# Two transformer layers on one core: a new order of the dense matmuls, zero matmuls in idle TensorE time, and smaller first loads

## The chip, the cores and the metric

The kernel runs on one core of a Trainium2 chip. The metric is the device time of one execution in microseconds (us), the median of several runs. A profile of one execution shows what each engine did: TensorE (PE: matmuls; PEld: its weight loads), VectorE (DVE), ScalarE (ACT), GpSimd (POOL) and SyncE (SP, which issues the DMA transfers). In lines of the profile, L672 means line 672 of that kernel's file.

## The reference

Four blocks follow one another on a stream x of 2048 tokens by 512 features: attention, token-mixing MLP, attention, MLP, that is two layers with the same weights.

```python
def _A_ref(x, wqkv, wo):                 # attention: 32 heads of 16, window of 256 tokens
    qkv = (x @ wqkv) ...                 # split in q, k, v per head
    scores = einsum("bhqd,bhkd->bhqk", q, k) * 16 ** -0.5
    mask = (i - j >= 0) & (i - j < 256)
    p = softmax(where(mask, scores, -1e9))
    return (p @ v) ... @ wo
def _B_ref(x, w1, b1, w2, b2):           # MLP over the token axis
    h = layernorm(x)
    u = gelu(einsum("bsd,sf->bdf", h, w1) + b1)      # 2048 tokens -> 1792
    y = einsum("bdf,fs->bds", u, w2) + b2            # 1792 -> 2048 tokens
    return y transposed
x = x + A(layernorm(x));  x = x + B(layernorm(x))
x = x + A(layernorm(x));  x = x + B(layernorm(x))
```

## The kernel before

The kernel is written as a graph of operations. Python code, before anything is compiled, gives each operation an estimated cost, plays the graph through on a simple model of the engines, and so fixes the order of instructions on each engine. The chip then runs those orders, with semaphores for the dependencies. An order is never changed while the kernel runs.

The tokens are worked in four chunks of 512. The steps of a layer are p (normalise, project q, k, v), a (attention), w (output projection), u (part of the first MLP matmul), U (the last part, with GELU):

```python
STEPS = ("p0 p1 a0 p2 w0 u0 a1 p3 w1 u1 a2 w2 u2 a3 w3 U3",
         "p0 p1 a0 p2 w0 a1 p3 w1 u01 a2 w2 u2 a3 w3 U3")
```

The second MLP matmul (y) of layer 0 is part of layer 1's p steps. TensorE takes scores first, then probabilities x V (PV), then dense matmuls by priority, which is their place in the program:

```python
        if e == "tensor":
            for kind in (SCORE, PV):
                c = [(o.prio, t, o) for t, o in est if o.kind == kind and t <= m + self.WINDOW[kind]]
                if c:
                    c.sort(key=lambda x: x[0])
                    return c[0][1], c[0][2]
...
    HOLD = 0.0
    WINDOW = {0: 100.0, 1: 150.0}
    SLACK = {"scalar": 60.0}
...
        STEP = 2                       # dense matmuls of a group that are issued as one operation
        def fprio():
            return 1e6 + len(g.ops)
```

Attention, for each of 4 groups of heads in a chunk, goes through 4 or 5 pieces. A piece is a set of score matmuls into four PSUM banks, two exponentials on ScalarE from PSUM to `pt`, and masks on VectorE. Score banks are limited to 6 of 8, so one and a half pieces fit:

```python
        psum = Pool("psum", 8, {"sc": 6, "small": 3, "big": 6})
...
                    prev_sc[0] = op("tensor", f_sc, reads=[tq] + kk, writes=[sa, sb_], ... kind=SCORE, mode="row", tag="sc")   # L672
                    for u, ts in ((0, sa), (1, sb_)):
                            return e.activation(pt[:, tp.slot, 2 * u:2 * u + 2, 0:n], PS[:, b0:b0 + 2, 0:n],               # L684
                                                ACTF.Exp, scale=SMSCALE)
                        ...                                                                                                 # masks: L697, L700
                op("tensor", f_pv, ... kind=PV, mode="pv", ...)                                                             # L717
```

The last group of heads of the last chunk uses another form of PV (L730). The results go through a normalisation by way of DRAM (cs, scr, rr, rscr, md), which ends in a product on GpSimd (L781).

The projections: K is copied from PSUM to `stg` by VectorE or ScalarE, and GpSimd spreads it to `kbd` in two operations (L604), the form the scores read:

```python
                op(*evac(lambda: stg[:, ts.slot, :], lambda: PS[:, ft.slot, :]), reads=[ft], writes=[ts], prio=-1e4)
                for h in range(2):
                    op("gpsimd", lambda e, h=h: e.tensor_scalar(
                        kbd[:, tk[o].slot, :, h, :], stg[:, ts.slot, :].rearrange("p (s n) -> p s n", n=64),
                        par[:, h:h + 1], 0.0, op0=ALU.mult, op1=ALU.add), ...)
```

Normalisation (`ln_block`): statistics of x (L530, L532) on VectorE, reciprocal root on GpSimd (L535, L537), and `xh_sb` on VectorE (L541). In the last chunk it is done for two tiles of 128 tokens at a time, and the first MLP matmul (L830) and the transposes (L579) wait for it:

```python
            ln_block([4 * m, 4 * m + 1], True)
            ln_block([4 * m + 2, 4 * m + 3], True)
```

The first loads:

```python
        load_x(0, 2)
        load_x(2, 4)
        load_w(1)
        load_w(0)
        load_x(4, 8)
        load_w(2)
        load_x(8, 12)
        load_x(12, 16)
```

Of the kernel before, what the change touches and what calls it, by code (L numbers as in the profile page):

```python
# [7 lines left out]
dt = mybir.dt  # L8
ALU = mybir.AluOpType
# [4 lines left out]
SWITCH = 95.0  # L14
SCORE, PV, DENSE = 0, 1, 2
STEPS = ("p0 p1 a0 p2 w0 u0 a1 p3 w1 u1 a2 w2 u2 a3 w3 U3",
# [24 lines left out]
class Op:  # L41
    __slots__ = ("idx", "eng", "engs", "fn", "cost", "lat", "prio", "deps", "users", "ndeps", "tiles", "start", "end",
                 "done", "seq", "dma", "extra", "kind", "mode", "tag")


class Graph:
# [15 lines left out]
    def op(self, eng, fn, reads=(), writes=(), cost=100.0, lat=None, prio=None, dma=False, after=(), holds=(),  # L62
           kind=DENSE, mode="full", tag=""):
# [6 lines left out]
        o.prio, o.kind, o.mode = prio, kind, mode  # L70
# [88 lines left out]
    def _pick(self, e, cand, ready, free, mode):  # L159
# [8 lines left out]
        for o in cand:  # L168
# [3 lines left out]
            t = max(ready[o.idx], t)  # L172
            if any(tl.slots is None for tl in o.tiles):
# [11 lines left out]
        if e == "tensor":  # L185
            for kind in (SCORE, PV):
                c = [(o.prio, t, o) for t, o in est if o.kind == kind and t <= m + self.WINDOW[kind]]
                if c:
                    c.sort(key=lambda x: x[0])
                    return c[0][1], c[0][2]  # L190
# [8 lines left out]
    HOLD = 0.0  # L199
    WINDOW = {0: 100.0, 1: 150.0}  # L200
    SLACK = {"scalar": 60.0}

    HAM = 3413.3

# [18 lines left out]
    def schedule(self):  # L223
        self.busy, self.rates = {}, [0.5]
# [12 lines left out]
        while left:  # L237
# [8 lines left out]
            m, e, o = best  # L246
            for x in o.engs:
                cand[x].remove(o)
            o.eng = e
            o.fn, o.cost = o.engs[e]  # L250
            self._alloc(o)
# [6 lines left out]
            else:  # L258
                if e == "tensor":
                    o.cost = self._clocked(m, o.cost)  # L260
                o.end = free[e] = m + o.cost
                o.done = o.end + (o.lat if o.lat is not None else self.LAT[e])
# [14 lines left out]
    def emit(self, block):  # L277
# [22 lines left out]
        pending = len(self.ops)  # L300
# [83 lines left out]
def bass_interleave_layers__sliding_block__mixer_token_mlp__prompt_kernel(  # L384
# [18 lines left out]
    NACT = 2  # L403
# [3 lines left out]
    with es:  # L407
# [21 lines left out]
        ident = sb("ident", [P, P])  # L429
        ldm = sb("ldm", [P, 2, 64])  # L430
# [30 lines left out]
        op("gpsimd", lambda e: e.memset(mhalf[:], -0.5), writes=["mhalf"])  # L461

# [7 lines left out]
        def load_x(t0, t1):  # L470
            op("sync", lambda e: e.dma_start(x_sb[:, t0:t1, :], x_src[:, t0:t1, :]),
               writes=[f"x{t}" for t in range(t0, t1)], dma=True, cost=(t1 - t0) * 600, prio=-1e6)

        def load_w(i):
            op("sync", lambda e: e.dma_start(wqkv[:, :, i * 512:(i + 1) * 512], w_src[:, :, i * 512:(i + 1) * 512]),
               writes=[f"w{i}"], dma=True, cost=2600, prio=-1e6)
        load_x(0, 2)
        load_x(2, 4)
        load_w(1)
        load_w(0)  # L480
        load_x(4, 8)
        load_w(2)
# [445 lines left out]
```

The softmax here doesn't subtract the row's maximum and nothing guards it: scores larger than these inputs give would overflow.

## Time and profile before

| | us |
|---|---|
| time, median of 3 runs | 501.48 (497.84 to 502.52) |
| span of the profiled execution | 499.8 |
| TensorE busy | 430.5 |
| VectorE busy | 377.1 |
| ScalarE busy | 321.9 |
| GpSimd busy | 137.0 |
| mean granted TensorE clock | 0.973 |

A busy share is an average over stages that differ. So the page has the span in 40 slices of 12.5 us, with a digit for the busy tenths of each engine in each. Idle times are listed with what ended them: "A <- B: total, times, longest" says how long A stood still until B was done. "issue" means that the profile shows nothing that the engine waited for.

### The profile page before, as it was taken

To read this page: it belongs to the slowest core of one execution; us is meant where nothing else is said; L and a number is where in the kernel's file an instruction comes from. 1 tells how busy PE (TensorE), PEld (TensorE's weight loads), DVE (VectorE), ACT (ScalarE), POOL (GpSimd) and SP (SyncE) were. 2 spreads that over 40 slices of the span, in tenths; PEclk is the share of its full clock that TensorE was granted. 3 is DMA by queue.
4 is the path that set the end of the run, shared out by engine and by line. 5 is a ranking of instruction groups with operands and counts; after the bars stand their busy time and mean duration, and the time that the engine had idled before them with its cause. 6 is when DMAs were issued, how large, how long until landed. Compare 5 with 4: busy or idle time off the path is not lost.

```text
span 499.8 us, 15471 instructions
## 1 busy us (share of the span) xinstructions
PE 430.5 (86%) x6746; PEld 209.0 (42%) x6816; DVE 377.1 (75%) x745; ACT 321.9 (64%) x365; POOL 137.0 (27%) x205
## 2 busy tenths in 40 slices
PE   2998758798859859699999899898889998999997
PEld 1554423344423334244544444345444344444443
DVE  6799957888888867766888878998897678872222
ACT  1788987898789961080598998697988872070000
POOL 3472333315431131102321621561481212100000
PEclk9999988899979979899999999999999999999999
DMA  8944243264326534154037355344534672524663
GB/s 266 216 98 146 100 148 110 95 199 134 104 102 202 176 101 119 39 147 125 24 117 226 113 163 164 111 142 126 162 96 153 200 220 75 147 64 118 197 193 103
DMA packets 91435, 69.23 MB, mean 139 GB/s; under 512 B 16232, under 2 KB 79848, under 8 KB 91368
## 3 DMA queue, kind: packets, MB, share of 16 engines
q1 hardware_dynamic: 91368, 68.25, 45.7%
q8 instruction: 53, 0.87, 0.8%
q14 instruction: 14, 0.11, 0.1%
HBM read 49.42 MB, written 18.32 MB: 136 GB/s over the span
## 4 chain that ended last, share of the span: by engine, by line
PE 50%; DVE 27%; ACT 9%; DMA 7%; POOL 2%; issue 2%; SPq 1%; POOLq 0%
PE PS L830 16%; PE PS L853 15%; ACT pt L684 9%; PE PS L717 5%; PE PS L595 5%; DVE stats L530 4%; PE PS L672 4%; DVE pt L700 3%; DVE xh_sb L541 3%; DVE pt L697 3%; DMA rr<-cs 3%; DVE cs L759 3%; PE PS L791 2%; DMA rscr<-rr 2%; DVE vt L567 2%
## 5 line engine op out<-in xcount | busy, mean ns | idle before, releaser
L684 ACT ACTIVATE pt<-PS 128x1024 bf16<-128x1024 f32 (+1 forms) x304 | 282.9, 1033 | 47.3 <-PE PS L672 43.0
L830 PE MATMUL PS<-xh_sb,w1b 128*128 128x512 bf16 x423 | 103.8, 387 | 17.2 <-DVE xh_sb L541 7.7
L853 PE MATMUL PS<-ub,w2b 128*128 128x512 bf16 x427 | 100.6, 380 | 2.7 <-issue 2.1
L781 POOL TENSOR_TENSOR oT<-md 128x512 bf16<-128x512 f32 x30 | 39.3, 1309 | 154.9 <-DMA md<-rscr 154.8
L672 PE MATMUL PS<-qT,kbd 32*128 32x64 bf16 (+4 forms) x1632 | 61.3, 246 | 19.6 <-ACT pt L684 9.1
L700 DVE TENSOR_TENSOR pt<-pt,ldm 128x1024 bf16<-128x1024 bf16 (+1 forms) x80 | 58.0, 726 | 16.2 <-ACT pt L684 16.1
L830 PEld LDWEIGHTS PS<-xh_sb,w1b 128*128 128x128 bf16 x448 | 40.4, 99 | 68.0 <-DVE xh_sb L541 13.4
L595 PE MATMUL PS<-xhT,wqkv 128*128 128x512 bf16 x239 | 62.5, 393 | 5.4 <-issue 2.8
L853 PEld LDWEIGHTS PS<-ub,w2b 128*128 128x128 bf16 x448 | 41.0, 98 | 50.6 <-issue 4.8
L604 POOL TENSOR_SCALAR kbd<-stg,par 128x512 bf16<-128x512 bf16 x64 | 50.0, 792 | 36.8 <-DVE stg L567 30.5
L672 PEld LDWEIGHTS PS<-qT,kbd 32*128 32x128 bf16 x1632 | 23.5, 93 | 77.8 <-ACT pt L684 52.5
L842 DVE TENSOR_TENSOR ub<-PS,ub 128x512 f32<-128x512 f32 x70 | 47.3, 688 | 10.5 <-PE PS L830 10.1
L858 DVE SCALAR_TENSOR_TENSOR x_sb<-PS,b2col,x_sb 128x512 bf16<-128x512 f32 x32 | 23.9, 748 | 40.1 <-PE PS L853 40.1
L697 DVE TENSOR_TENSOR pt<-pt,ldm 128x512 bf16<-128x512 bf16 (+1 forms) x104 | 43.6, 427 | 9.8 <-ACT pt L684 9.1
L845 ACT ACTIVATE ub<-ub,b1col 128x512 bf16<-128x512 f32 x28 | 19.6, 719 | 45.3 <-DVE ub L842 42.8
L717 PE MATMUL PS<-pt,vt 64*18 64x64 bf16 (+4 forms) x3040 | 42.1, 257 | 7.0 <-ACT pt L684 2.5
L530 DVE BATCH_NORM_STATS2 stats<-x_sb 128x6 f32<-128x512 bf16 x64 | 42.7, 681 | 2.9 <-DMA x_sb<-in_A_x_dram 2.5
L759 DVE COPY cs<-PS 128x512 f32<-128x512 f32 x60 | 38.5, 682 | 6.4 <-PE PS L717 6.2
L717 PEld LDWEIGHTS PS<-pt,vt 64*18 64x18 bf16 x3040 | 32.6, 89 | 19.5 <-ACT pt L684 10.7
L595 PEld LDWEIGHTS PS<-xhT,wqkv 128*128 128x128 bf16 x256 | 22.0, 100 | 32.7 <-issue 7.9
L541 DVE TENSOR_SCALAR xh_sb<-x_sb,agg,rstd 128x512 bf16<-128x512 bf16 x64 | 28.5, 476 | 8.8 <-POOL rstd L537 8.5
L791 PE MATMUL PS<-wo_sb,oT 128*128 128x512 bf16 x121 | 30.9, 381 | 3.7 <-DVE oT L748 1.3
(49 smaller groups left out, 297.4 us busy)
## 6 DMA issues: line engine op xcount, KB each, us to landing
scr<-cs SPq DMA_DIRECT2D x30, 512.0 KB, 3.2
w1b<-in_B_w_dram SPq DMA_DIRECT2D x56, 256.0 KB, 3.2
w2b<-in_B_w_dram SPq DMA_DIRECT2D x16, 896.0 KB, 6.3
md<-scr SPq DMA_DIRECT2D x60, 128.0 KB, 2.8
md<-rscr SPq DMA_DIRECT2D x60, 128.0 KB, 2.8
out_dram<-x_sb SPq DMA_DIRECT2D x16, 128.0 KB, 2.8
wqkv<-in_A_wqkv_dram SPq DMA_DIRECT2D x3, 512.0 KB, 7.7
x_sb<-in_A_x_dram SPq DMA_DIRECT2D x3, 512.0 KB, 9.5
```

The lines of the kernel that those rows point to most:

```text
L530: op("vector", lambda e, t=t: e.bn_stats(stats[:, t, :], x_sb[:, t, :]), reads=[f"x{t}"], writes=[f"st{t}"], cost=dve_cost(512))
L595: mm_group(ft, 4, lambda e, c: e.matmul(PS[:, ft.slot, :], lhsT=wqkv[:, c, which * 512 + o * P:which * 512 + (o + 1) * P], rhs=xhT[:, tx.s ...
L604: op("gpsimd", lambda e, h=h: e.tensor_scalar(kbd[:, tk[o].slot, :, h, :], stg[:, ts.slot, :].rearrange("p (s n) -> p s n", n=64), par[:, ...
L672: last = e.matmul(PS[:, bank(r), c0 * 64:(c0 + nb) * 64], lhsT=kbd[32 * r:32 * r + 32, tkk.slot, jj, :, :].rearrange("p h n -> p (h n)"), ...
L684: return e.activation(pt[:, tp.slot, 2 * u:2 * u + 2, 0:n], PS[:, b0:b0 + 2, 0:n], ACTF.Exp, scale=SMSCALE)
L697: return e.tensor_tensor(v, v, msk.unsqueeze(1).to_broadcast([P, 4, w]), op=ALU.mult)
L700: return e.tensor_tensor(v, v, msk.unsqueeze(1).unsqueeze(1).to_broadcast([P, 4, k, w]), op=ALU.mult)
L717: last = e.matmul(PS[32 * r:32 * r + 18, tO[h].slot, q0 * 64:(q0 + nb) * 64], lhsT=vt[64 * h:64 * h + 64, tvv.slot, jj, 4 * o + r, :], rhs ...
L759: op("vector", lambda e, tO=tO[h], tc=tc, h=h: e.tensor_copy(cs[:, tc.slot, h], PS[:, tO.slot, :]), reads=[tO[h]], writes=[(tc, h)], cost= ...
L830: out_ = e.matmul(PS[:, tu.slot, :], lhsT=w1b[:, tw.slot, s, tt * P:(tt + 1) * P], rhs=xh_sb[:, 4 * m + s, :], start=(n == 0 and s == 0), ...
L842: op("vector", lambda e, tu=tu, ft=ft: e.tensor_tensor(uacc(ft), PS[:, tu.slot, :], uacc(ft), op=ALU.add), reads=[tu] + uk(ft), writes=uk( ...
L853: mm_group(ft, NFT, lambda e, fc: e.matmul(PS[:, ft.slot, :], lhsT=w2b[:, tw.slot, fc, k * P:(k + 1) * P], rhs=uT(fc), start=(fc == 0), st ...
```

## The change

It does the following.

- The dense matmul groups get offsets to their priority from a table (`RANK`), which a search found on the model. The model itself is changed: [...]its windows and slacks are other ones. Dense matmuls are issued in fours instead of twos (singly in the last MLP part).
- 13 zero matmuls run ahead of the first real ones, and more are put where the model sees TensorE idle for long, to keep its clock up. In the order that results there are four of these, all in layer 0.
- x is first loaded in tiles of 128 KB, and the first weights in pieces of 128 KB, so that the first work can start sooner.
- K of chunk 0 in layer 0 goes from PSUM to `kbd` by ScalarE directly (`KACT`).
- The last chunk is normalised one tile at a time.
- Some set-up operations get other priorities and costs.

`EVACT` says the same as `NACT` did. With the values given here `XHP` (normalise on GpSimd), `NTR` and `DTR` (transposes by DMA) and `PVSPLIT` (PV in two parts) leave the kernel as it was.

```diff
-SWITCH = 95.0
+SWITCH = 100.0
+NWARM = 13
+NTR, DTR = 4, 1200
+EVACT = {(0, 0), (0, 1), (1, 0), (1, 1)}
+XHP = set()
+RANK = (
+    0, 0, 453, -32, -93, 0, -132, -49, 69, 0, 0, 0, 0, 0, 0, 0, -49, 7, 0, 52, -55, 0, -56, 46, 35, -50, -11, -39,
 ...  (322 numbers in all)
+KACT = {(0, 0, o) for o in range(4)}
+PVSPLIT = {True: ((0, 4),), False: ((0, 5),)}
 ...
+            if e == "vector" and o.port:
+                t = max(t, self.ported[1])
+            elif e == "gpsimd":
+                t = max(t, self.ported[0])
 ...
-            for kind in (SCORE, PV):
-                c = [(o.prio, t, o) for t, o in est if o.kind == kind and t <= m + self.WINDOW[kind]]
 ...
+            sc = [(o.prio, t, o) for t, o in est if o.kind == SCORE]
+            if sc:
+                _, t, o = min(sc, key=lambda x: x[0])
+                if t <= m + self.WINDOW[o.layer][0]:
+                    return t, o
+            pv = [(o.prio, t, o) for t, o in est if o.kind == PV and t <= m + self.WINDOW[o.layer][1]]
 ...
-    HOLD = 0.0
-    WINDOW = {0: 100.0, 1: 150.0}
-    SLACK = {"scalar": 60.0}
+    HOLD = 300.0
+    WINDOW = ({0: 100.0, 1: 300.0, 2: 50.0}, {0: 50.0, 1: 300.0, 2: 50.0})
+    SLACK = {"scalar": 60.0, "tensor": 300.0}
 ...
+            t = free["tensor"] + (SWITCH if mode != "full" else 0.0)
+            if e == "tensor" and self.warm and t + self.WARM[0] + (SWITCH if o.mode != "full" else 0.0) < m:
 ...  (puts a zero matmul there)
+        zset = op("vector", lambda e: e.memset(zero[:], 0.0), writes=["zero"], cost=120)
+        f_warm = lambda e, t: e.matmul(PS[:, t.slot, :], lhsT=zero[:], rhs=zero[:].unsqueeze(1).to_broadcast([P, 4, P]),
+                                       start=True, stop=True)
+        g.warm = (psum, f_warm, [zset])
+        for i in range(NWARM):
+            tw = Tile(psum, 1, "big")
+            op("tensor", lambda e, tw=tw: f_warm(e, tw), reads=["zero"], writes=[tw], cost=216, prio=-1e6)
 ...
-        load_x(0, 2)
-        load_x(2, 4)
-        load_w(1)
-        load_w(0)
+        load_x(0, 1)
+        load_x(1, 2)
+        load_w(4, 5)
+        load_x(2, 3)
+        load_x(3, 4)
+        load_w(0, 1)
+        load_w(8, 12)
+        load_w(5, 8)
+        load_w(1, 4)
         load_x(4, 8)
-        load_w(2)
         load_x(8, 12)
         load_x(12, 16)
 ...
-        STEP = 2
+        STEP = 4
+
+        groups = [0]
 
         def fprio():
-            return 1e6 + len(g.ops)
+
+            k = groups[0]
+            groups[0] += 1
+            return 1e6 + len(g.ops) + (RANK[k] if k < len(RANK) else 0) + 1e-4 * k
 ...
+                if kact:
+                    for h in range(2):
+                        op("scalar", lambda e, h=h: e.activation(
+                            kbd[:, tk[o].slot, :, h, :], PS[:, ft.slot, :].rearrange("p (s n) -> p s n", n=64), ACTF.Copy,
+                            scale=par[:, h:h + 1]), reads=[ft, ("par", h)], writes=[(tk[o], h)], cost=act_cost(512, 1),
+                           prio=-1e4)
+                    return
 ...
-            ln_block([4 * m, 4 * m + 1], True)
-            ln_block([4 * m + 2, 4 * m + 3], True)
+            for ts in ([[4 * m + i] for i in range(4)] if m == NC - 1 else [[4 * m, 4 * m + 1], [4 * m + 2, 4 * m + 3]]):
+                ln_block(ts, True)
 ...
-            cls = "big" if last else "small"
+            cls, st = ("big", 1) if last else ("small", STEP)
```

## The prediction

> **What bounds the kernel now.** I read the page from the top: the busy shares, then the slices, then the idle times of ScalarE and TensorE by what ended them, and last the stretches where those idle times sit.
>
> Busy shares and slices on the page:
>
> ```profile
> PE 430.5 (86%) x6746; PEld 209.0 (42%) x6816; DVE 377.1 (75%) x745; ACT 321.9 (64%) x365; POOL 137.0 (27%) x205
> ...
> PE   2998758798859859699999899898889998999997
> ...
> ACT  1788987898789961080598998697988872070000
> ...
> PEclk9999988899979979899999999999999999999999
> ```
>
> TensorE (PE) is busy 86% of 499.8 us, so 69 us are idle, and PEclk shows slices in which its clock was lowered. ScalarE (ACT) is dense only in two blocks, slices 1 to 14 and 20 to 32: the exponentials of layer 0 and of layer 1. What ScalarE waited for, over the whole run (total, times, longest):
>
> ```profile
> ACT pt L684 <- PE PS L672: 43.0, 44, 4.1
> ACT ub L845 <- DVE ub L842: 42.8, 3, 21.9
> ACT xhT L569 <- PE PS L579: 19.2, 4, 9.6
> ```
>
> The first line is the one that counts inside attention: the exponential (L684) lacks scores (L672). By stretch it is 10.7 us up to 100 us, 7.9 us from 100 to 184, 10.9 from 246 to 330 and 9.1 from 330 to 415. The other two fall outside attention.
>
> Busy time by stretch (columns: length, PE, weight loads, DVE, ACT, POOL with their counts, PE clock, DMA share, GB/s):
>
> ```profile
> 62.50:75.00 12.50, 7.04 (x186) 3.57 (x180) 6.40 (x12) 11.09 (x14) 4.45 (x6) 0.86 0.46 149
> 137.50:150.00 12.50, 7.05 (x185) 3.29 (x188) 10.17 (x22) 10.69 (x13) 3.92 (x6) 0.73 0.30 104
> 200.00:212.50 12.50, 7.63 (x30) 2.94 (x29) 9.04 (x21) 1.18 (x2) 1.89 (x4) 0.86 0.14 39
> 300.00:312.50 12.50, 11.79 (x243) 6.17 (x247) 10.83 (x21) 11.02 (x13) 1.83 (x3) 1.00 0.56 163
> 462.50:475.00 12.50, 12.39 (x58) 5.65 (x58) 3.00 (x4) 0.00 (x0) 0.00 (x0) 1.00 0.70 199
> ```
>
> So there are three regimes. In layer 0's attention (16.8 to 182 us) ScalarE leads: TensorE is short of filler and now and then half clocked. In layer 1's (242 to 411) PE and ACT are both near full. From 412 to 497 TensorE alone works, warm, and nothing but less work shortens it.
>
> Two more looks, from the timeline of all engines (start, length, what, idle before it and its releaser):
>
> ```profile
> 11.11 5.26 PE L595 MATMUL PS<-xhT,wqkv 128*128 128x512 bf16 x12 [0.52 <-DVE xhT L567]
> 16.76 1.94 ACT L684 ACTIVATE pt<-PS 128x1024 bf16<-128x1024 f32 x2 [1.43 <-PE PS L672]
> ```
>
> ```profile
> 179.41 1.26 POOL L781 TENSOR_TENSOR oT<-md 128x512 bf16<-128x512 f32 x1 [2.15 <-DMA md<-rscr]
> 179.54 1.68 DVE L700 TENSOR_TENSOR pt<-pt,ldm 128x1024 bf16<-128x1024 bf16 x1
> 183.33 0.63 PE L830 MATMUL PS<-xh_sb,w1b 128*128 128x512 bf16 x1 [3.99 <-DVE pt L697]
> 208.06 13.58 PE L830 MATMUL PS<-xh_sb,w1b 128*128 128x512 bf16 x55 [4.87 <-DVE xh_sb L541]
> 221.47 12.25 PE L853 MATMUL PS<-ub,w2b 128*128 128x512 bf16 x55
> ```
>
> The first projections take 438 ns each (5.26 / 12), later ones of the same size 223 ns at most (12.25 / 55; a record may be missing): the start is cold, though the clock column says 1.00 there. At the end of layer 0 TensorE stands still twice, 4.0 and 4.9 us.
>
> [...]in 1 us stretches the clock is 0.50 at about 67.3 to 70.7, 77.6 to 81, 91.3 to 94.6, 142.6 to 149.8, 180.5 to 187 and 207.7 to 211 us, that is 8 windows or 27 us, each after a gap; and 438 against 223 ns. [...]The mask of 1.68 us above, beside a GpSimd product of 1.26 us, against 0.66 us for the same mask alone[...]. [...]The first 256 KB of x landed 2.90 us after issue[...].
>
> **The change part by part.**
>
> *Start.* The change's thirteen zero matmuls of 512 columns run while nothing else can: at the cold 438 ns at most 5.7 us, from about 1 us on, over before the first transposes (7.40 us before the change, I expect about 6). The twelve projections then cost 12 x 0.216 = 2.6 us instead of 5.26: 2.6 us saved. The tiles of x come one by one ahead of most weights, so the last of four transposes' inputs is ready near 9.5 us instead of 11.05: 1.5 us. K of chunk 0 now goes from PSUM to kbd by two ScalarE operations instead of a copy and two GpSimd operations of 0.69 to 0.79 us: about neutral for the first one. First exponential near 12.7 instead of 16.76: about −4 us. Against it: ScalarE gets 8 kbd operations (I take 0.7 us, from the 0.719 us of L845, which also takes a value per partition) and loses net five copies of 0.59: 5.6 − 2.9 = +2.7 us in a stretch it leads.
>
> *Layer 0 attention.* ScalarE waits 18.6 us here (10.7 + 7.9). A piece of scores (0.40 us on PE) feeds two exponentials (2 x 1.045 = 2.09 us), so some 1.7 us of filler belong between two pieces. In the order of instructions before, there were 61 separate runs of scores for 76 pieces (15 pieces straight after another, PE idle), after there are 69 (7). Eight more gaps filled with about 1.5 us of dense work is 12 us of TensorE work that no longer delays a later piece; fewer idle stretches also means fewer half-clock windows. Of the five cold windows in this phase (17 us, with 13 us busy in it, so 6.5 us lost) I take half away. Some of both is the same time. I put the phase at −10 + 2.7 = −7.3 us.
>
> *End of layer 0.* The wait of 4.87 us for xh: normalisation of the last chunk is now one tile at a time, and 32 dense matmuls (6.9 us) lie between the first and the last output projection's use: I take off 4.5. The half clock at 180.5 to 187 and 207.7 to 211 stretched some 6.7 us of busy time: −2.5 of the possible 3.3. Twelve dense matmuls (2.6 us) now stand in the 4 us wait before the last probabilities x V: −2. Counting from the last scores of layer 0 to the first of layer 1, there are 18 fewer dense matmuls (−3.9 us) and 64 v matmuls more (64 x 59 ns by 2.37 us for 40, +3.8): nothing. Sum −9.
>
> *Layer 1.* TensorE is nearly the bound, so reordering moves work only. After the last scores there are 388 dense matmuls instead of 380 (+1.7 us); between first and last scores two dense ones more (+0.4) and the 64 v fewer (−3.8). PE idle in 242 to 412 is about 14 us; I take 4 of it. Sum −5.7.
>
> *Given back.* Mode changes of the array rise from 323 to 349, and I put 0.1 us on each (the timeline has 0.16 to 0.21 us of "issue" before dense matmuls at some of them, nothing at others): +2.6. Dense blocks of four matmuls (0.86 us) instead of two hold scores up longer: +1. Four zero matmuls in idle time: 0.9 us of time that was idle.
>
> Sum: −4 −7.3 −9 −5.7 +3.6 = −22.4, so 501.5 − 22.4 = 479.1. I say 480, since the parts add in full only if nothing else takes over.
>
> **Rivals.** *The order was fitted to a model, and the chip departs from it.* Engines keep a fixed order, so one late tile stalls all behind it. For it: I added up what stands between every two runs of scores (0.216 us a dense matmul, 0.059 a v, 0.065 a transpose, 1.4 us for 112 of PV, 0.1 a mode change). Gaps of over 1.75 us, too long for the exponentials, rise from 22 to 32 in layer 0 and from 31 to 42 in layer 1. Against it: the time by which all gaps exceed 1.7 us goes from 21.0 to 15.8 and from 24.3 to 26.6 us. Then only the start and the end of layer 0 gain: −4 −9 +3.6, about 492. *TensorE's total is the bound.* The work is the same matmuls plus 17; if layer 1 loses what layer 0 wins, through the later tail, the time would be 486 to 490. *ScalarE becomes the bound of layer 0*, by its +2.7 us: the phase then gains only 2 or 3 us, about 484. *All idle and cold time in attention goes*: 465 to 468.
>
> **Range and chances.** The first, pessimistic rival gives 492, the best one 465 to 468; 468 to 494 should hold it 8 times in 10. Faster by over 2% means under 491.4: 0.79. Within 2%: 0.17. Slower: 0.04, because the start and the 4.87 us wait are gains that hardly depend on the fit.
>
> **What would show it.** First exponential at 12 to 14 us and first projections at about 220 ns each; PE idle before the last chunk's L830-type matmuls of layer 0 under 1 us; half-clock windows down from 8 to 3 or fewer; the exponentials' wait for scores down from 43 to 30 us or less; PE busy down to 415 to 420. Wrong would be: the wait for scores unchanged or larger, or layer 1 longer from its first exponential to the end than the 257 us (499.8 − 242.3) of before.

## The result, and the profile after

The changed kernel takes 484.65 us (median of 3 runs, 483.38 to 485.62) against 501.48 before; the ratio is 0.968, with a 95% interval of 0.960 to 0.976. The profiled execution has a span of 483.9 us against 499.8.

The lines of its page that answer to those shown of before, busy shares and slices (a slice is now 12.1 us):

```profile
PE 444.7 (92%) x6833; PEld 207.6 (43%) x6833; DVE 373.5 (77%) x747; ACT 323.5 (67%) x368; POOL 131.9 (27%) x205
...
PE   7887978798979899999998999999999999999897
...
ACT  2899878989999961531898999699689860160000
...
PEclk8999988999999979999999999999999999999999
```

TensorE's busy time seems to have grown by 14 us, but that is no growth in work: the trace before lacks 70 of the 1,280 dense matmul records (423 of 448 for L830, for example), the trace after lacks none. The weight loads, 6,816 before and 6,833 after, differ by just the 17 zero matmuls. So I compare the ends of stretches, and busy sums with care.

What ScalarE waited for after the change (total, times, longest; L763 are now the scores, L775 the exponentials):

```profile
ACT pt L775 <- PE PS L763: 38.6, 41, 6.6
```

The line that I had called the one that counts went only from 43.0 to 38.6 us. It has to be split by stretch: in layer 0's attention the wait went from 18.6 to 12.9 us, in layer 1's from 24.4 to 25.7 (first scores of the layer included, 4.1 and 6.6 us of these). Here is layer 0's attention before, after, and in two kernels of the experiments below, e7 (without the table) and e10 (the order of before with zero matmuls):

```profile
ACT pt L684 <- PE PS L672: 18.6, 17, 2.8
ACT pt L775 <- PE PS L763: 12.9, 14, 2.6
ACT pt L763 <- PE PS L751: 13.1, 15, 1.9
ACT pt L687 <- PE PS L675: 13.8, 17, 1.9
```

So the fall from 18.6 us is no measure of the gain: e7 and e10 have most of the fall and next to nothing of the gain.

I cut the span at the first and the last exponential of each layer, from ScalarE's timeline:

| stretch, us | before | after | difference | predicted |
|---|---|---|---|---|
| start to first exponential | 16.76 | 17.03 | +0.3 | −4 |
| layer 0 attention | 165.66 | 160.91 | −4.8 | −7.3 |
| between the layers | 59.92 | 51.58 | −8.3 | −9 |
| layer 1 attention and after | 168.36 + 89.10 | 164.17 + 90.21 | −3.1 | −5.7 |
| given back, in no one stretch | | | | +3.6 |
| sum | 499.8 | 483.9 | −15.9 | −22.4 |

The start, from the timeline of all engines after (start, length, what, idle before it and its releaser):

```profile
1.04 4.90 PE L523 MATMUL PS<-zero 128*128 128x512 bf16 x13 [1.04 <-DVE one L572]
...
6.92 0.72 PE L662 MATMUL PS<-ident,xh_sb 128*128 128x128 bf16 x8 [0.99 <-DVE xh_sb L612]
...
7.70 0.89 DVE L612 TENSOR_SCALAR xh_sb<-x_sb,agg,rstd 128x512 bf16<-128x512 bf16 x2
8.49 3.52 PE L709 MATMUL PS<-wqkv,xhT 128*64 128x256 bf16 x32 [0.85 <-DMA wqkv<-in_A_wqkv_dram]
...
11.95 0.62 PE L662 MATMUL PS<-ident,xh_sb 128*128 128x128 bf16 x8
...
13.13 2.76 PE L679 MATMUL PS<-xhT,wqkv 128*128 128x512 bf16 x12 [0.56 <-DVE xhT L646]
```

The projections (last line) are warm now, 230 ns each. But the second pair of transposes, whose inputs were ready at 8.59 us, stands behind 32 v matmuls in TensorE's order and runs only at 11.95; and those v matmuls take 110 ns each instead of 59, because the clock was 0.50 from 8.4 to 11.8 us.

Between the layers, the same view of TensorE:

```profile
175.88 2.86 PE L923 MATMUL PS<-xh_sb,w1b 128*128 128x512 bf16 x12
178.89 1.28 PE L821 MATMUL PS<-pt,one 128*32 128x128 bf16 x56 [0.16 <-DVE pt L788]
...
183.22 2.85 PE L923 MATMUL PS<-xh_sb,w1b 128*128 128x512 bf16 x12 [0.97 <-DMA w1b<-in_B_w_dram]
185.90 1.03 PE L884 MATMUL PS<-wo_sb,oT 128*128 128x512 bf16 x4
186.77 1.98 PE L923 MATMUL PS<-xh_sb,w1b 128*128 128x512 bf16 x8
...
193.86 12.91 PE L923 MATMUL PS<-xh_sb,w1b 128*128 128x512 bf16 x56
```

Twelve dense matmuls now stand where TensorE waited 4.0 us, and the last 56 (L923) start with no wait where they had waited 4.87 us, as the output projections (L884) are spread among first-MLP matmuls. The stretch as a whole, busy times before and then after (columns as in the tables above: length, PE, weight loads, DVE, ACT, POOL, clock, DMA share, GB/s):

```profile
182.40:242.30 59.90, 53.73 (x350) 24.84 (x358) 39.93 (x73) 15.59 (x22) 7.90 (x16) 0.93 0.36 102
```

```profile
177.90:229.50 51.60, 50.33 (x393) 23.95 (x392) 37.60 (x69) 14.50 (x22) 10.31 (x22) 1.00 0.40 114
```

The −8.3 us are 4.9 us less idle PE (6.2 to 1.3) and 3.4 us less busy PE; the clock was 0.93 before and is 1.00. (Eight matmul records are missing before, 350 of 358, so up to 8 x 0.216 = 1.7 us of its idle time were work. With before's order and no record missing, e6 is idle for 5.3 us here.)

Part of this is work that moved. The weight loads, of which no record is missing, count the matmuls in each stretch: 27 dense ones fewer here (218 before, 191 after), of which 19 went into layer 0's attention (276 to 295), 7 to the time after the last exponential (372 to 379) and 1 to layer 1's attention (402 to 403); and 60 v matmuls more, which were in layer 1's attention before (252 there, now 192). At 0.22 us a dense matmul (12.25 / 55 before) and 0.06 a v (1.94 / 32 in e3), I estimate that this makes 5.9 − 3.6 = 2.3 of the 8.3 us.

One stall of the profile after has no releaser. Five of the twelve matmuls of a piece of scores run, then TensorE stands still, in the midst of an operation that has no wait in it:

```profile
67.15 0.36 PE L763 MATMUL PS<-qT,kbd 32*128 32x128 bf16 x5
...
69.33 0.34 PE L763 MATMUL PS<-qT,kbd 32*128 32x320 bf16 x7 [1.81 <-issue]
```

After it the clock is halved from 69.8 to 76.6 us.

### The profile page after: what moved, and what is told of

It is laid out like the page before. It is cut to its first block, busy times and chain, and to the rows that moved or that the text cites. A ratio compares the mean times of both kernels' runs of the same rounds, so it can differ in the third digit from the quotient of the medians.

```text
span 483.9 us, 15575 instructions
## 1 busy us (share of the span) xinstructions
PE 444.7 (92%) x6833; PEld 207.6 (43%) x6833; DVE 373.5 (77%) x747; ACT 323.5 (67%) x368; POOL 131.9 (27%) x205
## 4 chain that ended last, share of the span: by engine, by line
PE 52%; ACT 25%; DVE 13%; DMA 7%; issue 2%; POOL 1%; SPq 1%
ACT pt L775 23%; PE PS L923 15%; PE PS L946 15%; PE PS L808 5%; PE PS L679 5%; PE PS L763 5%; PE PS L709 3%; PE PS L884 3%; DVE cs L852 2%; DVE pt L791 2%; DMA w1b<-in_B_w_dram 2%; DMA w2b<-in_B_w_dram 2%; DVE pt L788 1%; DVE stats L601 1%; ACT kbd L688 1%
## 5 line engine op out<-in xcount | busy, mean ns | idle before, releaser
L775 ACT ACTIVATE pt<-PS 128x1024 bf16<-128x1024 f32 (+1 forms) x304 | 283.7, 1029 | 39.2 <-PE PS L763 38.6
L923 PE MATMUL PS<-xh_sb,w1b 128*128 128x512 bf16 x448 | 108.3, 385 | 2.6 <-DMA w1b<-in_B_w_dram 1.3
L946 PE MATMUL PS<-ub,w2b 128*128 128x512 bf16 x448 | 103.6, 380 | 1.3 <-DMA w2b<-in_B_w_dram 1.3
L763 PE MATMUL PS<-qT,kbd 32*128 32x64 bf16 (+4 forms) x1632 | 61.8, 247 | 21.6 <-ACT pt L775 9.0
L791 DVE TENSOR_TENSOR pt<-pt,ldm 128x1024 bf16<-128x1024 bf16 (+1 forms) x80 | 59.0, 738 | 11.5 <-ACT pt L775 10.8
L679 PE MATMUL PS<-xhT,wqkv 128*128 128x512 bf16 x256 | 63.9, 385 | 2.1 <-DVE qT L646 0.6
L923 PEld LDWEIGHTS PS<-xh_sb,w1b 128*128 128x128 bf16 x448 | 39.5, 98 | 58.3 <-issue 6.8
L946 PEld LDWEIGHTS PS<-ub,w2b 128*128 128x128 bf16 x448 | 41.0, 98 | 52.1 <-issue 4.5
L763 PEld LDWEIGHTS PS<-qT,kbd 32*128 32x128 bf16 x1632 | 23.4, 93 | 80.2 <-ACT pt L775 51.4
L695 POOL TENSOR_SCALAR kbd<-stg,par 128x512 bf16<-128x512 bf16 x56 | 42.9, 779 | 43.4 <-DVE stg L646 37.7
L788 DVE TENSOR_TENSOR pt<-pt,ldm 128x512 bf16<-128x512 bf16 (+1 forms) x104 | 41.7, 413 | 6.5 <-ACT pt L775 5.9
L808 PE MATMUL PS<-pt,vt 64*18 64x64 bf16 (+4 forms) x3040 | 39.2, 244 | 3.4 <-DVE pt L788 1.5
L606 POOL TENSOR_SCALAR rstd<-agg 128x2 f32<-128x2 f32 (+1 forms) x40 | 9.5, 237 | 107.5 <-DVE agg L603 104.4
L709 PE MATMUL PS<-wqkv,xhT 128*64 128x256 bf16 x512 | 36.4, 285 | 1.2 <-DMA wqkv<-in_A_wqkv_dram 0.9
L808 PEld LDWEIGHTS PS<-pt,vt 64*18 64x18 bf16 x3040 | 30.8, 85 | 14.4 <-DVE pt L788 7.2
```

Of the source, the lines that this page charges most:

```text
L679: mm_group(ft, 4, lambda e, c: e.matmul(PS[:, ft.slot, :], lhsT=wqkv[:, c, which * 512 + o * P:which * 512 + (o + 1) * P], rhs=xhT[:, tx.s ...
L709: last = e.matmul(PS[64 * hf:64 * hf + 64, ft.slot, sc * 256:(sc + 1) * 256], lhsT=xhT[:, tx.slot, c, tok:tok + 64], rhs=wqkv[:, c, 1024:1 ...
L763: last = e.matmul(PS[:, bank(r), c0 * 64:(c0 + nb) * 64], lhsT=kbd[32 * r:32 * r + 32, tkk.slot, jj, :, :].rearrange("p h n -> p (h n)"), ...
L788: return e.tensor_tensor(v, v, msk.unsqueeze(1).to_broadcast([P, 4, w]), op=ALU.mult)
L791: return e.tensor_tensor(v, v, msk.unsqueeze(1).unsqueeze(1).to_broadcast([P, 4, k, w]), op=ALU.mult)
L808: last = e.matmul(PS[32 * r:32 * r + 18, tO[h].slot, q0 * 64:(q0 + nb) * 64], lhsT=vt[64 * h:64 * h + 64, tvv.slot, jj, 4 * o + r, :], rhs ...
```

## The experiments

Theory: the gain is the order that the search found, which puts dense work where TensorE had stood idle, in layer 0's attention and between the layers. Rivals: it is the array's clock (zero matmuls, fewer gaps); it is the other changes to the model and the kernel (windows, fours, single tiles). Two more questions are why the start gave nothing, and whether it can. "Orders kept" means that the orders of the instructions were taken as the kernel named has them and only the edit shown was made to them; otherwise the scheduler ran again and moved other work too. Ratios are to the kernel before timed in the same rounds, where its median was 498.42 us for e1 to e4, 500.57 for e5 to e8 and 499.24 for e9 to e12. In the rounds of e9 to e12 the changed kernel was run again (e11), and is 14.7 us faster (6 runs against 27); the 16.8 us of the result are from 3 runs each.

| kernel | median us | ratio (95%) | first exp. | layer 0 att. | between | layer 1 att. | tail | clock |
|---|---|---|---|---|---|---|---|---|
| before | 501.48 | | 16.76 | 165.66 | 59.92 | 168.36 | 89.10 | 0.973 |
| after | 484.65 | 0.968 (0.960 to 0.976) | 17.03 | 160.91 | 51.58 | 164.17 | 90.21 | 0.982 |
| e1 no zeros | 480.74 | 0.963 (0.957 to 0.970) | 17.57 | 161.72 | 50.72 | 164.50 | 88.19 | 0.986 |
| e2 transposes first | 487.45 | 0.975 (0.970 to 0.981) | 14.05 | 162.52 | 51.84 | 163.70 | 90.19 | 0.993 |
| e3 more zeros | 481.60 | 0.964 (0.959 to 0.970) | 15.70 | 158.36 | 52.12 | 164.16 | 88.66 | 0.996 |
| e4 both | 481.81 | 0.964 (0.959 to 0.969) | 14.10 | 161.41 | 52.38 | 163.06 | 88.65 | 0.993 |
| e5 before, zeros | 500.58 | 1.000 (0.997 to 1.004) | 16.54 | 162.36 | 59.42 | 168.57 | 90.91 | 0.968 |
| e6 before, single tiles | 499.64 | 0.999 (0.996 to 1.002) | 16.06 | 165.57 | 61.01 | 167.12 | 88.54 | 0.976 |
| e7 no table | 497.55 | 0.996 (0.992 to 1.000) | 14.61 | 160.59 | 60.53 | 174.17 | 91.00 | 0.976 |
| e8 pairs of tiles | 488.86 | 0.977 (0.972 to 0.982) | 15.72 | 164.58 | 53.79 | 164.63 | 89.68 | 0.990 |
| e9 table, layer 0 only | 483.79 | 0.973 (0.967 to 0.979) | 15.60 | 160.04 | 49.62 | 163.27 | 92.47 | 0.989 |
| e10 before, zeros in gaps | 498.11 | 0.999 (0.997 to 1.001) | 16.72 | 160.44 | 61.32 | 167.74 | 89.08 | 0.986 |
| e11 after again | 484.52 | 0.972 (0.967 to 0.977) | 17.21 | 160.96 | 50.46 | 163.06 | 90.71 | 0.986 |
| e12 more zeros again | 482.63 | 0.968 (0.964 to 0.972) | 15.50 | 160.75 | 51.62 | 162.90 | 89.53 | 0.996 |

The stretches and the clock are of the one profiled execution of each kernel, the medians of all its runs. One kernel's runs differ by 1% and more: those of before beside e9 to e12 span 495.5 to 503.9 us, and the six of e11 go from 481.97 us (at a clock of 0.996) to 487.81 (at 0.982).

Stretches scatter too. The four kernels with the order of before (before, e5, e6, e10) take 160.4 to 165.7 us in layer 0's attention, and the five with the changed order (after, e1, e3, e11, e12) 158.4 to 161.7; e3 and e12 are one kernel, at 158.4 and 160.8. So the 4.8 us of layer 0's attention are not shown. Between the layers the four take 59.4 to 61.3 us and the five 50.5 to 52.1, in layer 1's attention 167.1 to 168.6 and 162.9 to 164.5: these two differences stand clear of the scatter. The tail, 88.5 to 90.9 and 88.2 to 90.7, has none.

**e1: no zero matmuls.** Orders kept.

```diff
+        zeros = {o.idx: o for o in g.order["tensor"] if 5 <= o.idx <= 17 or o.idx < 0}
+        for o in g.ops + g.dummies:       # whoever waited for a zero matmul's bank waits for what it waited for
+            while any(d.idx in zeros for d in o.extra):
+                o.extra = [y for d in o.extra for y in (zeros[d.idx].extra if d.idx in zeros else [d])]
+        g.order["tensor"] = [o for o in g.order["tensor"] if o.idx not in zeros]
 ...
```

> The changed kernel's orders, instruction for instruction, with all 17 zero matmuls left out. If the zeros at the start keep the clock up where it counts, the first twelve projections fall back from 230 ns to about 438 ns, the first exponential moves from 17.0 to about 19.5 us and the time rises by 2 to 4 us (487 to 488). If they cool off again before they are of use (the granted clock was 0.50 from 8.3 to 11.7 us with them), the time changes by under 1 us.

Measured 480.74 us, ratio 0.963. The first exponential came 0.5 us later (17.57), and the projections still took about 230 ns each: in either kernel the 32 v matmuls ahead of them run at half clock (3.63 us here, 3.52 with the zeros), and the projections after them do not. So the 17 zero matmuls as they stand bring nothing that these runs can see. The time is even lower than with them, where I had expected it within 1 us; the intervals of the two ratios overlap, and the stall at 67 us, told of under e11 and e12, is shorter here.

**e2: transposes first.** Orders kept; the banks stay as they were.

```diff
 ...  (start(engine, old, new) puts the operations, by number, in a new order)
+        start("tensor", [81, 83, 94, 95, 97, 98, 87, 85, 89, 111, 92, ...],      # tr tr v v v v tr tr K0 K1 Q0 ...
+              [81, 83, 87, 85, 89, 92, 97, 98, 181, 111, 94, 95, ...])          # tr tr tr tr K0 Q0 v v scores K1 v v ...
+        start("scalar", [84, 96, 88, ...], [84, 88, 90, 91, 93, 182, 183, ...])   # evacuations in the same order
+        start("vector", [99, 86], [86, 99])
```

> The changed kernel's orders with only the first instructions moved: the last two transposes of chunk 0 and the first K and Q ahead of the 32 v matmuls. Theory of the order (the start was lost because v stands ahead of the second transposes, whose inputs were ready at 8.6 us but which ran at 11.95): first exponential at 13 to 14.5 us instead of 17.0, time 481 to 483. Theory of the clock (it was lost because the clock was halved from 8.3 to 11.7 us): the projections now run in that cold window at 438 ns, first exponential at 15.5 us or later, time 483.5 to 484.5.

The first exponential moved from 17.03 to 14.05 us, as the theory of the order has it, and the time did not follow: 487.45 us, ratio 0.975 (0.970 to 0.981). ScalarE's timeline of this kernel, and then of the changed one at the same exponentials:

```profile
14.05 1.94 ACT L775 ACTIVATE pt<-PS 128x1024 bf16<-128x1024 f32 x2 [1.41 <-PE PS L763]
15.87 1.27 ACT L688 ACTIVATE kbd<-PS,par 128x512 bf16<-128x512 f32 x2
17.01 0.61 ACT L648 CAST vt<-PS 128x512 bf16<-128x512 f32 x1
17.66 1.94 ACT L775 ACTIVATE pt<-PS 128x1024 bf16<-128x1024 f32 x2
...
27.59 1.95 ACT L775 ACTIVATE pt<-PS 128x1024 bf16<-128x1024 f32 x2
```

```profile
17.03 3.77 ACT L775 ACTIVATE pt<-PS 128x1024 bf16<-128x1024 f32 x4
...
28.00 2.06 ACT L775 ACTIVATE pt<-PS 128x1024 bf16<-128x1024 f32 x2
```

A lead of 3.0 us at the first exponential is 0.4 us at 28 us. In the changed kernel ScalarE had spread K for the second group of heads and evacuated v before its first exponential; here it does that between the first and the second pair. Most of the lead was thus work put in another order, and the first exponential is no measure of the start; a later one is better. By the exponentials that the changed kernel starts at 66.03 us, e2 is 1.0 us ahead, so a third of its lead did last.

**e3: more zeros.** Orders kept.

```diff
 ...  (more(at, banks) puts a zero matmul for each bank ahead of operation `at`)
+        more(81, (0, 1, 2, 3))      # four zero matmuls ahead of the first transposes, into these banks
+        more(94, (1, 2, 3, 4))      # four between the first transposes and v
```

> The changed kernel's orders with eight more zero matmuls, four after the first thirteen and four between the first transposes and v. Theory of the clock: no half clock from 8.3 to 11.7 us, the 32 v matmuls take 1.9 instead of 3.52 us, first exponential at about 15.4 us, time 482.5 to 483.5. Theory of the order: the second transposes still wait for v, the gain is at most 1.6 us.

TensorE's timeline of this kernel:

```profile
8.75 1.94 PE L709 MATMUL PS<-wqkv,xhT 128*64 128x256 bf16 x32 [0.60 <-DMA wqkv<-in_A_wqkv_dram]
```

The half clock at the start is gone, v takes 1.94 us, and most of this lead keeps: the first exponential is at 15.70 (−1.33), the exponentials at 50.15 us of the changed kernel are at 48.78 (−1.37), and those at 66.03 us at 65.18 (−0.85; −1.08 in e12, the same kernel). Median 481.60 us, ratio 0.964.

**e4: both.**

> Both edits of the two runs before at once. If both causes count, first exponential at 12.5 to 13.5 us and time 480 to 481.5, that is most of the 4 us that the prediction had for the start. If the exponentials of chunk 0 are held up elsewhere (VectorE, loads), the first exponential moves but the time stays within 1.5 us of 484.65.

Measured 481.81 us, ratio 0.964, the same as e3; at 66 us it is 1.04 us ahead of the changed kernel. Either edit alone brings about 1 us by then (e2, e3), and both together no more; the 4 us predicted for the start are not to be had this way.

**e5: the kernel before, with 13 zero matmuls at the front.** Orders kept.

```diff
+        zs = [op("tensor", lambda e, i=i: e.matmul(PS[:, i % 8, :], lhsT=zero[:], rhs=..., start=True, stop=True),
+                 reads=["zero"]) for i in range(13)]
 ...
+        g.order["tensor"][:0] = zs
```

> The kernel before with nothing but 13 zero matmuls ahead of its first transposes. If the array then stays warm until its first projections at 11.1 us, these take 2.6 instead of 5.26 us, the first exponential moves from 16.8 to about 14.2 and the time falls by 2 to 2.6 us. If it cools off again in the gaps between the transposes (as it did in the changed kernel), the first exponential stays within 0.6 us of 16.8 and the time does not move.

Ratio 1.000 (0.997 to 1.004). Its profile has the twelve projections (here L596) at 423 ns each:

```profile
11.08 5.08 PE L596 MATMUL PS<-xhT,wqkv 128*128 128x512 bf16 x12 [0.52 <-DVE xhT L568]
```

The zeros end at 6.23 us, 1.16 us before the first transposes; with these alone between zeros and projections the array was cold again, at a clock of 0.50 from 9.0 to 15.8 us.

**e6: the kernel before, last chunk normalised one tile at a time.**

```diff
-            ln_block([4 * m, 4 * m + 1], True)
-            ln_block([4 * m + 2, 4 * m + 3], True)
+            for ts in ([[4 * m + i] for i in range(4)] if m == NC - 1 else [[4 * m, 4 * m + 1], [4 * m + 2, 4 * m + 3]]):
+                ln_block(ts, True)
```

> The kernel before with only the last chunk of each layer normalised one tile at a time; TensorE's order stays the same. If the wait of 4.87 us at the end of layer 0 was the two-tile grain, it falls to about 2.5 us and the half clock after it may go: time down by 2 to 4 us. If it was where the dense matmuls stand (all of them ahead of the last output projection), the wait stays above 4 us and the time does not move.

Ratio 0.999 (0.996 to 1.002), TensorE's order unchanged. The wait stays (TensorE's timeline of this kernel):

```profile
206.82 7.35 PE L830 MATMUL PS<-xh_sb,w1b 128*128 128x512 bf16 x20 [4.55 <-DVE xh_sb L541]
```

As long as 14 of the 16 output projection matmuls come last of all, the whole chain of the first tile lies open: addition, statistics, root, xh.

**e7: the table empty.**

```diff
-RANK = (0, 0, 453, -32, -93, ...)
+RANK = ()
```

> The changed kernel with the table of priorities empty, so that the dense groups stand as the new model places them without the search; all else as changed. If the search is the main part of the gain: 490 us or more and clock back to 0.975 or less. If the model's other changes (windows, port, fours, zeros, single tiles) made it: 486 us or less. I expect 488.

497.55 us, ratio 0.996 (0.992 to 1.000): without the search nearly nothing is left of the gain, though all else of the change is there. Its timeline of TensorE between the layers (L872 output projection, L911 first MLP) is that of before in small:

```profile
177.93 1.29 PE L809 MATMUL PS<-pt,one 128*32 128x128 bf16 x56 [3.19 <-DVE pt L776]
...
193.83 3.62 PE L872 MATMUL PS<-wo_sb,oT 128*128 128x512 bf16 x16
200.33 2.49 PE L911 MATMUL PS<-xh_sb,w1b 128*128 128x512 bf16 x6 [2.89 <-DVE xh_sb L600]
```

And in layer 1's attention, which is 10 us longer than with the table, stands this (L667 projection, L796 PV, L934 second MLP, L763 here the exponentials):

```profile
320.47 1.04 PE L667 MATMUL PS<-xhT,wqkv 128*128 128x512 bf16 x4 [0.31 <-DVE qT L634]
321.34 3.71 PE L872 MATMUL PS<-wo_sb,oT 128*128 128x512 bf16 x16
...
324.98 1.37 PE L796 MATMUL PS<-pt,vt 64*18 64x128 bf16 x112
...
326.28 1.90 PE L934 MATMUL PS<-ub,w2b 128*128 128x512 bf16 x8
326.39 1.94 ACT L763 ACTIVATE pt<-PS 128x1024 bf16<-128x1024 f32 x2 [7.61 <-PE PS L796]
```

From 318.3 to 328.1 us TensorE does other work without one piece of scores, and ScalarE stands still for 7.6 us. All these waits for scores and PV add up to 34.1 us in this layer (26.5 and 7.6), against 25.7 in the changed kernel.

Layer 0's attention, though, is as short without the table (160.59 us) as with it (160.91 and 160.96 in e11). What the table does there is to put more into it: 295 dense matmuls in place of 280, by the weight loads. The table was not run on the old model, so what it would be worth without the other changes is open.

**e8: the changed kernel with pairs of tiles**, the diff of e6 turned round.

> The changed kernel with the last chunk normalised two tiles at a time, as before; the scheduler then also places the work around it differently. If the single tiles removed the wait at the end of layer 0, a wait of 1 to 3 us comes back ahead of the last first-MLP matmuls and the time rises by 1 to 3 us; if the order alone removed it, the stretch from the last exponential of layer 0 to the first of layer 1 stays at 51.6 us within 0.7.

488.86 us, ratio 0.977. A wait of 1.3 us for xh is back ahead of the last first-MLP matmuls, and the stretch between the layers takes 2.2 us more (53.79, where the changed order takes 50.5 to 52.1). Layer 0's attention is 3.7 us longer in this profile too; as the scheduler ran again, I can't put that down to the tiles.

**e9: the table for layer 0 alone.**

```diff
-            return 1e6 + len(g.ops) + (RANK[k] if k < len(RANK) else 0) + 1e-4 * k
+            return 1e6 + len(g.ops) + (RANK[k] if k < 136 else 0) + 1e-4 * k
```

> The changed kernel with only the first 136 numbers of the table, those of layer 0's dense groups; layer 1's stand as the model places them. Without any table the time was 497.6 us: 9 us more between the layers and 10 us more in layer 1's attention than with it. If the two layers' shares are what those stretches say: layer 0 ends as in the changed kernel (last exponential to first of layer 1 about 52 us), layer 1's attention takes about 174 instead of 164 us, time 490 to 496.

My expectation for layer 1 was wrong. 483.79 us, ratio 0.973, where the full table had 0.972 in the same rounds. Layer 1's attention takes 163.3 us without any number of its own. So layer 1's 10 us of e7 were no lack of priorities there. They go with the order that the scheduler found from where layer 0 left the model: TensorE's longest time without scores in layer 1's attention is 9.8 us in e7 and 4.3 in e9. Why it found the worse one was not followed up. The table's gain, as far as these runs show, comes from its first 136 numbers.

**e10: the kernel before, with zero matmuls in the gaps between pieces of scores.** Orders kept; 51 matmuls more.

```diff
+            if o.kind == SCORE and k and g.order["tensor"][k - 1].kind == SCORE:
+                sa = next(t for t in o.tiles if t.cls == "sc")
+                for i in range(3):
+                    z = op("tensor", lambda e, b=sa.slots[i % 2]: e.matmul(PS[:, b, :], lhsT=zero[:], ...), reads=["zero"])
+                    z.extra = list(g.was[id(sa)])       # waits for the former users of that bank alone
 ...
```

> The kernel before, its orders kept, with three zero matmuls in each of the 17 places where one piece of scores follows straight on another; they write the banks that the second piece will write, which come free about 1 us before it can start. It adds 51 matmuls and fills nothing useful, so it changes the clock alone. If the half-clock windows are a large part of what the change removed: clock from 0.973 to 0.985 or more and 3 to 6 us less. If the useful filler is what counts: time within 2 us of before, whatever the clock.

The clock rose from 0.973 to 0.986 in the profile (0.980 to 0.990 in its 20 runs, 0.965 to 0.982 in the 27 of before), and the ratio is 0.999 (0.997 to 1.001). The exponentials after these 17 places wait at most 0.2 us longer than in the kernel before, so the zeros did not hold ScalarE up; whether they delayed TensorE's other work was not separated. Raising the clock nearly as far as the change did (0.982 to 0.996 in its runs), with nothing useful in the gaps, gained about 1 us by the medians and at most 1.7 by the interval, what the zeros themselves cost included. The clock alone is not the main gain.

**e11 and e12: the changed kernel, and e3 once more, in the same rounds.**

> The changed kernel once more, on the same chip and in the same rounds as the next one: 484 us within 2.

> The changed kernel with the eight more zero matmuls at the start once more. The 1.3 us by which its first exponential came earlier was still there at 50 us, so 1.3 us less than the changed kernel in the same rounds, 481 to 483 us; if that is lost later, no difference.

484.52 and 482.63 us, ratios 0.972 (0.967 to 0.977) and 0.968 (0.964 to 0.972). The intervals overlap, so by time alone this is open. The first exponential is 1.7 us earlier once more (15.50 against 17.21).

These runs also tell where the stall at 67 us belongs. It parts the same piece of scores, five matmuls before and seven after, in after, e2, e8, e9 and e11, which all have 13 zero matmuls at the front: 1.81, 1.47, 1.54, 1.70 and 1.69 us. With 13 fewer instructions ahead (e1) a stall of 0.42 us comes 13 matmuls later; with eight more (e12) one of 0.41 us comes eight earlier, parting four transposes:

```profile
69.88 0.69 PE L763 MATMUL PS<-qT,kbd 32*128 32x64 bf16 x18 [0.42 <-issue]
```

```profile
66.24 0.33 PE L662 MATMUL PS<-ident,xh_sb 128*128 128x128 bf16 x3 [0.41 <-issue]
```

(e1 above, e12 below.) So it is bound to a place in TensorE's stream of instructions and not to what is computed there. Counting all of TensorE's instructions in the trace from the start (matmuls, weight loads and those of its sequencer), 1,985 stand ahead of it in each of these seven, and also in e5 (2.09 us, in the midst of PV) and e7 (0.79 us), which have other orders (in e1 and e2 eight matmul records are missing up to there). And in all fourteen kernels the next instruction starts 1.2 to 1.7 us after the seventh 16 KB packet of the queue that carries instructions (q8 on the page) has ended: in the changed kernel this packet runs from 67.05 to 68.11 us and TensorE goes on at 69.33; in e3 it ends at 64.27, TensorE gets there only at 65.89 and does not stall. So the stall fits instructions that come late. It was not tested by an edit made for it, and why the packet comes when it does was not looked into.

After the stall the kernels differ by more than the start had given: the exponentials that the changed kernel and e11 start at 80.45 and 80.48 us are at 75.63, 75.43 and 75.82 in e3, e4 and e12, and at 78.56 in e1. This would explain why these four have the lower medians (480.7 to 482.6, against 483.8 to 488.9 for after, e2, e8, e9 and e11); it is not shown to. e3 is the version that I would keep, though its lead over the changed kernel is no more than these 2 us.

## Why the prediction was right, and where it was not

The time of 484.65 us lies 4.65 above the 480 predicted and within 468 to 494. By the predicted steps:

- *What bounds it: three regimes, and TensorE short of filler in layer 0.* Right in kind: layer 0's attention holds 19 more dense matmuls after than before (276 to 295) and 15 more than without the table (280 in e7), and takes only 0.3 us longer than e7's; the stretch after it has so much less to do. But two of the measures do not show this. Runs of scores in layer 0 are 61 before, 69 after and 62 in e7, by the orders of instructions, and ScalarE's wait for scores there is 18.6, 12.9 and 13.1 us: e7 has the runs of before, and the wait of after. Filling gaps paid with useful work; e10, which fills them with zeros, got about 1 us.
- *Start, −4 us: wrong, +0.3.* This is the step that failed, and it is 4.3 of the 6.5 us by which the sum was off. Its first term held, as the projections became warm, but not through the zeros (about 230 ns each without them in e1, 423 ns with them in e5). Its second term, the last of four tiles ready near 9.5 us instead of 11.05, failed: the 11.05 us are when before's last tile had been transposed and copied. After, that tile was normalised by 8.59 us, but transposed only at 11.95 and copied by 13.07. I had read when the tiles of x come, and not that 32 v matmuls stand between the two pairs of transposes, which can be seen in the order. The smaller first load brought the first statistics of x from 3.71 to 3.13 us. And the measure was wrong: e2 brings the first exponential 3 us forward, and 1.0 us of this is left at 66 us. What the start could give was about 1 us, by the order (e2) or by the half clock on v (e3).
- *Layer 0 attention, −7.3: not shown; −4.8 in this pair of profiles.* The order of before takes 160.4 to 165.7 us here in four profiles, and before's own is the longest, so most of the 4.8 us may be scatter. The prediction put 12 us of filler into eight more gaps; the weight loads show 19 dense matmuls more, about 4 us, and 40 v matmuls fewer, and their worth appears in the next stretch. Five half-clock windows lay here before, four after. ScalarE's own work in this stretch grew by 1.0 us (146.1 to 147.1), not by 2.7, since more of it lies ahead of the first exponential.
- *End of layer 0, −9: right, −8.3*, made of waits, half clock and moved work as taken apart above. I had taken the moved work as nothing, and it is some 2 us (counted from exponential to exponential, which is not quite the stretch that I had counted). What removed the wait of 4.87 us was the spreading of the output projections: single tiles without it leave 4.55 us (e6), pairs with it leave 1.3 (e8).
- *Layer 1, −5.7, and +3.6 given back: −3.1 measured.* The 64 v matmuls fewer came about (60 in this cut), 3.6 us by the estimate above, and they are nearly the whole 4.2 us of layer 1's attention. The 4 us of PE idle did not: 31 matmul records are missing before. With before's order and no record missing, e6 is idle for 8.5 us here, as is the changed kernel (e6, then after; length, PE busy, and the rest as above):

```profile
242.64:409.75 167.11, 158.61 (x3034) 74.84 (x3032) 140.70 (x277) 144.67 (x159) 57.53 (x76) 1.00 0.50 148
```

```profile
229.52:393.69 164.17, 155.72 (x2972) 72.36 (x2971) 139.01 (x284) 143.68 (x156) 55.00 (x74) 1.00 0.48 148
```

- *The cost of mode changes* was misread in the same way: the 0.16 to 0.21 us of "issue" are missing records, since the traces of after and of e5 have none of them before dense matmuls. So most of the +3.6 given back had no ground, and it was luck that it brought the sum nearer to what was measured.
- *The clock column's 1.00 at the start* is no reading: the trace of before has no clock event before 16.2 us, and the first projections took 438 ns there.
- *The rival of the badly fitted order* did not come about for the order as a whole. *ScalarE as the bound of layer 0* did not as it was put: ScalarE still stands idle for 13.8 of the 160.9 us. But its number, 2 or 3 us for this stretch and about 484 in all, can't be told apart from what was measured.
- Of the signs named, the first exponential (17.03), half-clock windows (8 to 5, not to 3), the wait for scores (38.6, not 30 or less) and the busy sum missed; the last was unusable for want of records. The first projections (230 ns), the wait ahead of the last first-MLP matmuls (none) and the time from layer 1's first exponential to the end (254.4, under 257) came as said.

## What to carry to other kernels

A list of priorities that a search found on a model was worth some 2.4% on the chip here (ratio 0.996 without it, 0.972 with it): it moved dense work out of the stretch between the layers and spread what a chain waited for. Look at the order for blocks between two services of the waiting engine, such as 4 + 16 + 112 + 8 matmuls in a row, and for a chain's first step queued last. Before a difference between two profiles is explained, see how far the same order scatters in that stretch, and whether matmuls and weight loads agree in number; count what work each stretch holds. Judge a start not by its first important instruction but by a later one, after all set-up work is done. Zero matmuls kept the array warm at the start only where they ran nearly up to the real work (in e3 v starts 0.60 us after the last of them and takes 1.94 us; in e5, where 1.16 us lie between, the clock was 0.50 from 9.0 us), and a warmer clock in time that was a wait anyway gained about 1 us (e10).

## What the runs showed of the hardware

A stall of TensorE of up to 1.8 us (2.1 in e5) can belong to a place in its instruction stream: shift the stream by 13 or 8 instructions and it moves by just these. It lay behind 1,985 instructions in nine kernels, and in all fourteen TensorE passed this place 1.2 to 1.7 us after the same packet of instructions had ended. The array got warm and cold again within 12 us: in the changed kernel the zero matmuls start 0.43 us apart from 1.04 to 4.85 us and 0.22 us apart from 5.12 on, up to 5.94; then come eight transposes and 0.99 + 0.85 us of idle time, and from 8.4 to 11.8 us the clock was 0.50. From 5.94 to 8.4 us TensorE was busy for 0.7 of 2.5 us and never idle for over 0.99 us (in e5, from the end of the zeros at 6.23 to 9.0 us, for 0.8 of 2.8 us, and 1.16 us). With eight zero matmuls more the clock stayed at 1.00 there (e3: v in 1.94 instead of 3.52 us). In the kernel before, the granted clock is shown as 1.00 at the start, where the trace has no clock event up to 16.2 us, while the first projections take 438 ns and later ones 223 at most. And one program's time moves by over 1% from run to run: e11 from 481.97 us at a clock of 0.996 to 487.81 us at 0.982, though the clock does not tell all, as three of its runs at 0.986 take 484.10, 484.93 and 487.63 us.
